# One more batch of block products with seven multiplications, four more pairs with float32 numerators, and other buffer limits in a planned attention and MoE kernel

## The chip, the cores and the metric

The kernel runs on one core of a Trainium2 chip. The metric is the time of one execution on the device in microseconds (us). TensorE (PE in the profile) multiplies matrices, VectorE (DVE), ScalarE (ACT) and GpSimd (POOL) do the elementwise work, and all large transfers are issued from the queue of SyncE (SP).

## The reference

For each of 8 batches and 8 heads (576 rows, 64 columns) the reference computes attention with random features, and passes the result, as 4608 tokens of 512 values, through two matrix products with an activation between them:

```python
proj = np.einsum('bhsd,md->bhsm', x, omega)          # q and k, 128 features
h = proj - sum(x * x) / 2;  phi = np.exp(h - max(h)) / np.sqrt(128)
kv = np.einsum('bhsm,bhsd->bhmd', k_p, v);  z = np.sum(k_p, axis=2)
num = np.einsum('bhsm,bhmd->bhsd', q_p, kv);  den = q_p . z + 1e-06
x = num / den                                        # 4608 x 512
h = x @ w_in                                         # 512 -> 2048
g = h * erf(log(1 + exp(h)))
out = g @ w_out                                      # 2048 -> 512
```

All of it is float32.

## The kernel before, in words

**Work.** Attention goes by pairs of heads, four pairs to a batch, numbered 0 to 31 (pair 4b + p is pair p of batch b; its tiles are called `..._b_p`). For a pair, TensorE projects keys (`ppk`) and queries (`ppq`), VectorE takes row maxima, ScalarE exponentiates into `fk` and `fq`, TensorE makes `kvp` (keys by values) from `fk`, and turns `fq` by three groups of transpositions (`pt`). The turned queries are copied out of PSUM to `qh`, the pair's key values to `kh`, and the products `nd` of both hold numerators and denominators, which are divided into `xs`.

From there the MoE part takes over, batch by batch. A batch has two phases of 1024 hidden columns; a phase has four granules of the first product (`h...`, 256 hidden columns each) and four column blocks of the second product (`o...`, 128 output columns each). A column block belongs to the phase before the one in whose span it stands, so the second product runs one phase behind the first.

**Split numbers.** Most products are made with float32r operands that are split into a high and a low part: a product then takes three matmuls (high by high, high by low, low by high). Weights lie in tiles `w` as pairs of parts, activations in `xh` and `xl`, gated values in `gh` and `gl`, turned queries in `qh` and `ql`, key values in `kh` and `kl`.

**First product, two forms.** In batches below `PLAIN` (lines 301 to 302 set it and `WHOLE`) `plain1` (line 609) makes a granule's four output blocks from two block products each: 8 block products of 6 matmuls, 48 in all, and each output is copied out of PSUM. From batch `PLAIN` on, `gemm1` (line 622) makes them from seven block products in Strassen's manner: 42 matmuls, and each block that leaves PSUM is added to others (`h_add`, line 960; 7 additions and one copy to a granule). That form needs sums of weight blocks, which `make_sums` (line 407) computes once, in the batch `PLAIN - 1`, from the tiles which are there anyway: it restores the whole weights (`R`), adds and subtracts blocks (`S`), splits the sums (`cS`) and stores them to DRAM, from where they are fetched as `wS`. It also needs differences of activation blocks (`xc`), made by `split` (line 545) at a batch's start.

**Numerators, two forms.** For pairs below `WHOLE`, `kh` and `qh` are plain float32, there are no low parts, and `nd` is one float32 matmul; from pair `WHOLE` on, they are split, and `nd` is three matmuls (`attend`, line 919).

**Weights.** The weights come packed as int64 and must be rebuilt once: each tile is loaded (`st`), shifted and joined on the engines (`wt`, `pw`), split into `w`, and stored (`wdw`). All later uses fetch it from DRAM. This happens in batch 0 for the first product, and one phase behind it for the second, so the last of it lies in the first half of batch 1.

**Order.** No loop of the program sets the order of the instructions. `build` writes a list of operations with due times, and `Plan.order` (line 134) simulates the engines with fixed costs and puts out one order for each of them; each engine then runs its own in order and waits on semaphores. Buffers are slots of pools (`SLOTS`, line 61), and `CAPS` limits how many slots of its pool a stream of tiles may hold at once: `st` for loaded weights and `S` (in the pool of `gl`, 6 slots), `wt` for half-made weights and `R` (in the pool of `gh`, 6 slots), `att` for the attention's PSUM tiles and `moe1`, `moe2` for those of the MoE products (8 PSUM slots together). The first four pairs have a limit of their own, 7.

```python
def weights1(b, ph, fp):                                  # lines 430 to 434
    if b < PLAIN:
        t0, t1 = (unit(("1", ph, 2 * fp + i)) for i in range(2))
        if b == PLAIN - 1:
            make_sums(ph, fp, t0, t1)
whole = n < WHOLE                                         # lines 497 and 508
if held[t.stream] + k >= (t.cap or caps.get(t.stream, 99)):   # in order()
    return False
(plain1 if b < PLAIN else gemm1)(b, ph, x)                # line 722
```

`PLAIN` also enters the due times of the phases (lines 334 and 716) and three limits: tiles `w` may take 6 of 8 slots, and `gh` and `gl` 4 of 6, until a phase that is named by `PLAIN`.

## Time and profile before

| | |
|---|---|
| median of three executions | 1088.04 us (1085.89 to 1089.02) |
| profiled execution | 1085.2 us, its span 1083.2 us |
| PE busy | 1066.8 us, 98% of the span |
| DVE, ACT, POOL busy | 724.0, 672.6, 462.6 us |
| moved by DMA | 231.27 MB, mean 213 GB/s |
| granted TensorE clock | 0.999 |

Busy times are unions of instruction spans. Matmuls overlap in their pipeline, so the mean of a matmul (298 ns) is longer than the distance from one to the next. A row of the timeline gives the start, the length, the engine, the source line (all operations of this kernel have the one line of a helper, L755, so that the tiles' names tell them apart), and in brackets how long the engine had been idle and for whom. The batches' spans, by the first matmul of their first granule, begin near 49, 172, 299, 435, 575 and 705 us, and then every 130 us.

### The profile page before, as it was taken

The page shows a single profiled execution, that of the slowest core. Times are in us where ns is not written, and L with a number is a line of the kernel's source. Part 1 is how long each engine was busy: PE and PEld are TensorE (multiplying, and loading weights), DVE is VectorE, ACT ScalarE, POOL GpSimd, SP SyncE. Part 2 cuts the span into 40 slices and gives each one's busy share as a digit, 9 for nine tenths or more (in the row PEclk, how much of TensorE's full clock was granted, in tenths as well). Part 3 has the DMA queues.
Part 4 walks back from the last instruction along what each step waited for, and adds up shares of the span by engine and source line. Part 5 has one row for each costly group of instructions (what it writes and reads, how often), then busy time and mean ns, then how long its engine had stood idle before and what let it go on. Part 6 is the DMA issues. An engine that isn't in the chain of part 4 may idle for free.

```text
span 1083.2 us, 21493 instructions
## 1 busy us (share of the span) xinstructions
PE 1066.8 (98%) x8272; PEld 1059.2 (98%) x8272; DVE 724.0 (67%) x1302; ACT 672.6 (62%) x1262; POOL 462.6 (43%) x362
## 2 busy tenths in 40 slices
PE   7899999999999999999999999999999999999998
PEld 7799999999999999999999999999999999999998
DVE  5999988683585676946667565766657757565541
ACT  7768876576676685647647555675556665564440
POOL 5436336352294673815335334452435412253300
PEclk9999999999999999999999999999999999999999
DMA  8465676676367676568765766667765766667771
GB/s 235 162 210 177 221 265 223 227 274 200 115 218 240 225 234 202 177 206 255 226 208 183 248 226 223 187 211 233 230 210 182 241 203 197 216 229 265 264 240 52
DMA packets 70117, 231.27 MB, mean 213 GB/s; under 512 B 8288, under 2 KB 8672, under 8 KB 70016
## 3 DMA queue, kind: packets, MB, share of 16 engines
q1 hardware_dynamic: 69952, 229.84, 64.9%
q8 instruction: 66, 1.08, 0.4%
q14 instruction: 35, 0.29, 0.1%
q0 software_dynamic: 64, 0.07, 0.0%
HBM read 195.26 MB, written 34.60 MB: 212 GB/s over the span
## 4 chain that ended last, share of the span: by engine, by line
PE 94%; DVE 4%; ACT 1%; issue 0%; DMA 0%; DVEq 0%; POOLq 0%
PE o L755 37%; PE h L755 14%; PE hS L755 12%; PE hA L755 9%; PE ppk L755 6%; PE ppq L755 6%; PE kvp L755 5%; PE nd L755 5%; PE pt L755 2%; DVE mxk L755 0%; DVE xl L755 0%; DVE pw L755 0%; DVE gl L755 0%; DVE xc L755 0%; DVE qh L755 0%
## 5 line engine op out<-in xcount | busy, mean ns | idle before, releaser
L755 PE MATMUL o<-gh,w 128*128 128x288 f32 x2048 | 442.3, 298 | 1.9 <-DVE ql L755 1.0
L755 PEld LDWEIGHTS o<-gh,w 128*128 128x128 f32 x2048 | 338.3, 188 | 2.5 <-PE o L755 1.2
L755 PE MATMUL o<-gl,w 128*128 128x288 f32 x1024 | 301.8, 295 | 0.0
L755 PEld LDWEIGHTS o<-gl,w 128*128 128x128 f32 x1024 | 192.7, 188 | 0.1
L755 PE MATMUL h<-xh,w 128*128 128x288 f32 x768 | 176.0, 303 | 0.6 <-DVE hs L755 0.6
L755 PE MATMUL hS<-xh,wS 128*128 128x288 f32 x640 | 160.0, 299 | 1.1 <-DVE u L755 1.1
L755 POOL TENSOR_TENSOR hs<-gs,hs 128x576 f32<-128x576 f32 x64 | 101.4, 1607 | 105.7 <-ACT gs L755 68.9
L755 POOL TENSOR_TENSOR gl<-hs,gh 128x576 fp32r<-128x576 f32 x66 | 117.9, 1810 | 33.0 <-ACT gh L755 25.7
L755 PEld LDWEIGHTS h<-xh,w 128*128 128x128 f32 x768 | 129.1, 188 | 1.5 <-DVE hs L755 0.8
L755 ACT ACTIVATE fk<-ppk,mxk 128x128 f32<-128x128 f32 x288 | 82.2, 375 | 74.8 <-DVE mxk L755 74.5
L755 PE MATMUL hA<-xh,w 128*128 128x288 f32 x480 | 122.8, 300 | 0.0
L755 ACT ACT_TABLE_LOAD x91 | 116.8, 1283 | 4.3 <-DVE hs L755 2.0
L755 PEld LDWEIGHTS hS<-xh,wS 128*128 128x128 f32 x640 | 112.9, 188 | 1.3 <-DVE u L755 1.3
L755 POOL TENSOR_TENSOR uq<-uq 64x576 f32<-64x576 f32 x42 | 49.7, 1201 | 150.3 <-DMA uq<-qT 105.3
L755 PE MATMUL h<-xl,w 128*128 128x288 f32 x384 | 113.0, 294 | 0.0
L755 ACT ACTIVATE fq<-ppq,mxq 128x128 f32<-128x128 f32 x288 | 81.6, 372 | 30.4 <-DVE mxq L755 30.2
L755 DVE TENSOR_REDUCE mxk<-ppk 128x3 f32<-128x384 f32 x96 | 52.4, 555 | 62.6 <-PE ppk L755 61.3
L755 PE MATMUL hS<-xl,wS 128*128 128x288 f32 x320 | 94.2, 294 | 0.0
L755 POOL TENSOR_TENSOR uk<-uk 64x576 f32<-64x576 f32 x46 | 52.4, 1159 | 86.1 <-DMA uk<-kT 60.8
L755 PEld LDWEIGHTS hA<-xh,w 128*128 128x128 f32 x480 | 85.5, 188 | 0.1
L755 DVE TENSOR_TENSOR os<-o,os 128x288 f32<-128x288 f32 x64 | 29.0, 455 | 83.5 <-PE o L755 83.5
L755 PE MATMUL ppk<-wk,uk 128*128 128x128 f32 x576 | 78.1, 280 | 4.1 <-DVE wk L755 4.0
(94 smaller groups left out, 2084.6 us busy)
## 6 DMA issues: line engine op xcount, KB each, us to landing
w<-wdw SPq DMA_DIRECT2D x184, 512.0 KB, 4.4
wS<-wdcS SPq DMA_DIRECT2D x80, 512.0 KB, 4.0
st<-w SPq DMA_DIRECT2D x32, 512.0 KB, 4.5
wdw<-w SPq DMA_DIRECT2D x32, 512.0 KB, 4.2
v<-vP SPq DMA_DIRECT2D x32, 325.0 KB, 3.6
w<-wdw SPq DMA_DIRECT2D x40, 256.0 KB, 3.5
out<-os SPq DMA_DIRECT2D x32, 288.0 KB, 3.5
uk<-kT SPq DMA_DIRECT2D x31, 288.0 KB, 3.8
```

The lines of the kernel that those rows point to most:

```text
L755: return tc.keep_in_program_order(method(*args, **kwargs))
```

## The change

Three constants are set to other values, and the limits of three streams. Batch 2 is computed with seven block products to a granule in place of eight, the sums of weights are made in batch 1 in place of batch 2, pairs 8 to 11 get float32 numerators, loaded and half-made weights may hold three slots each in place of two, and the attention four PSUM tiles in place of five.

```diff
-CAPS = dict(st=2, wt=2, cv=2, att=5, moe1=3, moe2=2)
+CAPS = dict(st=3, wt=3, cv=2, att=4, moe1=3, moe2=2)
...
-WHOLE = 8
-PLAIN = 3
+WHOLE = 12
+PLAIN = 2
```

Since a planner sets the order, these lines move instructions everywhere from the first 15 us on. Counted over the whole program, by form: PE has 48 MoE matmuls fewer and 32 `nd` matmuls fewer (for 16 `nd` products, one float32 matmul in place of three); DVE has 56 additions `hs` and `u` of batch 2 more, 12 `ql` and 8 `kl` fewer; SP has 16 fetches more (16 of `wS` with 512 KB and 8 of `w` with 256 KB more, 8 of `w` with 512 KB fewer). Three places show how rows moved.

DVE in batch 1, first phase, around the copy that empties a block of granule 0 (`h111_0_0`). Before:

```order
L755 CAST gh0_1_2_2223<-hs0_1_2_1587 128x1152
L755 COPY os0_3_2237<-o0_0_3_0_2111 128x288
L755 TENSOR_TENSOR gl0_1_2_2242<-hs0_1_2_1587,gh0_1_2_2223 128x1152
L755 COPY hs1_0_0_2252<-h011_0_0_2219 128x288
L755 TENSOR_TENSOR xs_2_0_2285<-nd_2_0_0_0_2209,rc_2_0_0_2257 64x288
L755 TENSOR_TENSOR xs_2_0_2285<-nd_2_0_1_0_2233,rc_2_0_0_2257 64x288
L755 COPY hs1_0_0_2252<-h111_0_0_2278 128x288
```

and now:

```order
L755 TENSOR_TENSOR R0_1_2205<-w1_0_3_28_2097 128x512
L755 TENSOR_REDUCE mxk_2_1_2232<-ppk_2_1_1_2228 128x3
L755 TENSOR_TENSOR S0_1_2259<-R0_1_2205 128x256
L755 TENSOR_REDUCE mxk_2_1_2232<-ppk_2_1_2_2255 128x3
L755 COPY qh_2_0_2284<-pt_2_0_0_2264 128x384
L755 TENSOR_TENSOR hs0_1_3_1876<-gs0_1_3_2055,hs0_1_3_1876 128x1152
L755 TENSOR_TENSOR S0_1_2259<-R0_1_2205,S0_1_2259 128x256
L755 COPY hs1_0_0_2203<-h111_0_0_2216 128x288
L755 TENSOR_TENSOR cS0_1_0_2324<-S0_1_2259,cS0_1_0_2324 128x2x256
```

Sums of weights (`R`, `S`, `cS`) now stand between the attention's maxima and copies of pairs 8 and 9 and the copies of batch 1's blocks; there is no `ql` row for pair 8.

PE at pair 10 (`_2_2`), in batch 1. Before, from the last transposition on (the first `nd` of the pair follows one matmul after these rows):

```order
L755 MATMUL pt_2_2_2_3121<-ident_67,fq_2_2_2793 128x128 x3
L755 MATMUL h001_1_1_3091<-xh1_1_1976,w1_1_2_43_2902 128x288
L755 MATMUL h001_1_1_3091<-xl1_1_2014,w1_1_2_43_2902 128x288
L755 MATMUL h001_1_1_3091<-xh1_1_1976,w1_1_2_43_2902 128x288
L755 MATMUL h001_1_1_3091<-xh1_0_1966,w1_1_2_43_2902 128x288
L755 MATMUL h001_1_1_3091<-xl1_0_1988,w1_1_2_43_2902 128x288
L755 MATMUL h001_1_1_3091<-xh1_0_1966,w1_1_2_43_2902 128x288
L755 MATMUL h011_1_1_3137<-xh1_0_1966,w1_1_2_43_2902 128x288
L755 MATMUL h011_1_1_3137<-xl1_0_1988,w1_1_2_43_2902 128x288
L755 MATMUL h011_1_1_3137<-xh1_0_1966,w1_1_2_43_2902 128x288
L755 MATMUL h001_1_1_3091<-xh1_1_1976,w1_1_2_43_2902 128x288
L755 MATMUL h001_1_1_3091<-xl1_1_2014,w1_1_2_43_2902 128x288
```

and now:

```order
L755 MATMUL kvp_2_2_2842<-v_2_2_2031,fk_2_2_2671 128x65 x4
L755 MATMUL ppk_2_3_0_2866<-wk_71,uk_2_3_2589 128x128 x3
L755 MATMUL ppk_2_3_1_2875<-wk_71,uk_2_3_2589 128x128 x3
L755 MATMUL ppk_2_3_2_2883<-wk_71,uk_2_3_2589 128x128 x3
L755 MATMUL pt_2_2_0_2888<-ident_67,fq_2_2_2818 128x128 x3
L755 MATMUL pt_2_2_1_2903<-ident_67,fq_2_2_2818 128x128 x3
L755 MATMUL pt_2_2_2_2913<-ident_67,fq_2_2_2818 128x128 x3
L755 MATMUL nd_2_2_0_0_2922<-qh_2_2_2899,kh_2_2_2870 128x288
L755 MATMUL o0_1_2_0_2925<-gh0_1_0_2127,w2_1_2_0_37_2805 128x288
```

The attention of pair 10 now stands in one piece, with no MoE matmul between transpositions and `nd`; pair 11 has a like place.

PE at pair 18 (`_4_2`), in batch 3. Before:

```order
L755 MATMUL pt_4_2_2_6381<-ident_67,fq_4_2_6087 128x128 x3
L755 MATMUL nd_4_2_0_0_6386<-qh_4_2_6363,kh_4_2_6159 128x288
L755 MATMUL nd_4_2_0_0_6386<-ql_4_2_6368,kh_4_2_6159 128x288
L755 MATMUL nd_4_2_0_0_6386<-qh_4_2_6363,kl_4_2_6170 128x288
L755 MATMUL nd_4_2_1_0_6400<-qh_4_2_6363,kh_4_2_6159 128x288
L755 MATMUL nd_4_2_1_0_6400<-ql_4_2_6368,kh_4_2_6159 128x288
L755 MATMUL nd_4_2_1_0_6400<-qh_4_2_6363,kl_4_2_6170 128x288
```

and now:

```order
L755 MATMUL pt_4_2_2_6378<-ident_67,fq_4_2_6113 128x128 x3
L755 MATMUL nd_4_2_0_0_6383<-qh_4_2_6362,kh_4_2_6155 128x288
L755 MATMUL nd_4_2_0_0_6383<-ql_4_2_6367,kh_4_2_6155 128x288
L755 MATMUL nd_4_2_0_0_6383<-qh_4_2_6362,kl_4_2_6166 128x288
L755 MATMUL hS43_1_0_6393<-xh3_0_5300,wS_1_0_1_131_6092 128x288
L755 MATMUL hS43_1_0_6393<-xl3_0_5328,wS_1_0_1_131_6092 128x288
L755 MATMUL hS43_1_0_6393<-xh3_0_5300,wS_1_0_1_131_6092 128x288
```

After these rows twelve more MoE matmuls follow before the second `nd` of the pair: 15 matmuls stand now between the two where none did.

## The prediction, as it was made before the run

> **What bounds the kernel now.** I read the page first, for the bound.

> ```profile
> span 1083.2 us, 21493 instructions
> PE 1066.8 (98%) x8272; PEld 1059.2 (98%) x8272; DVE 724.0 (67%) x1302; ACT 672.6 (62%) x1262; POOL 462.6 (43%) x362
> PE 94%; DVE 4%; ACT 1%; issue 0%; DMA 0%; DVEq 0%; POOLq 0%
> ```

> TensorE is busy for 98% of the span and holds 94% of the chain that ended last; DVE, the next one, has a third of the span free. Only 16.4 us are not PE's, so what shortens PE's own list shortens the kernel. Then the busy times by stretch, at the start, and by batch:

> ```profile
> 0.00:20.00 20.00, 15.85 (x105) 15.05 (x106) 8.08 (x20) 15.69 (x39) 11.43 (x17) 1.00 0.85 220
> 20.00:40.00 20.00, 17.15 (x127) 15.09 (x127) 19.40 (x40) 14.93 (x48) 8.84 (x10) 1.00 0.66 195
> 40.00:60.00 20.00, 18.52 (x146) 17.24 (x145) 19.16 (x40) 15.04 (x44) 9.68 (x12) 1.00 0.49 162
> ...
> 172.00:299.00 127.00, 127.00 (x998) 127.00 (x997) 80.89 (x140) 81.18 (x161) 49.09 (x39) 1.00 0.59 201
> 299.00:435.00 136.00, 136.00 (x1069) 136.00 (x1069) 93.67 (x142) 93.20 (x182) 86.76 (x70) 1.00 0.67 224
> 435.00:575.00 140.00, 137.34 (x1071) 136.36 (x1070) 94.84 (x169) 84.53 (x155) 66.11 (x45) 1.00 0.66 211
> 575.00:705.00 130.00, 130.00 (x1023) 129.98 (x1022) 85.93 (x167) 79.59 (x147) 53.68 (x39) 1.00 0.68 217
> ...
> 1005.00:1035.00 30.00, 30.00 (x230) 30.00 (x229) 14.12 (x29) 9.51 (x11) 8.99 (x6) 1.00 0.79 272
> ```

> Columns: stretch, length, busy PE, weight load, DVE, ACT, POOL (with counts), clock, DMA share, GB/s. PE's idle time lies in the first 60 us (4.15 + 2.85 + 1.48 = 8.5 us), in batch 3 (435 to 575: 2.7 us) and at the end; in batches 1, 2 and 4 it is zero. The clock is full, so no stretch hides a throttle. Last, what PE waited for, and where, by the waits and the timeline:

> ```profile
> PE ppk L755 <- DVE wk L755: 4.0, 1, 4.0
> PE nd L755 <- DVE qh L755: 1.9, 2, 1.0
> PE hS L755 <- DVE u L755: 1.1, 1, 1.1
> PE o L755 <- DVE ql L755: 1.0, 1, 1.0
> ...
> 21.27 2.22 PE L755 MATMUL kvp<-v,fk 128*128 128x130 f32 x18 [0.84 <-ACT fq L755]
> 27.44 0.72 PE L755 MATMUL nd<-qh,kh 128*128 128x288 f32 x2 [0.90 <-DVE qh L755]
> 28.86 0.97 PE L755 MATMUL nd<-qh,kh 128*128 128x288 f32 x3 [0.70 <-ACT fk L755]
> ...
> 444.08 0.37 PE L755 MATMUL o<-gh,w 128*128 128x288 f32 x1 [1.02 <-DVE ql L755]
> 452.93 0.40 PE L755 MATMUL hS<-xh,wS 128*128 128x288 f32 x1 [1.09 <-DVE u L755]
> 517.97 0.40 PE L755 MATMUL nd<-qh,kh 128*128 128x288 f32 x1 [0.18 <-ACT qh L755]
> 518.74 0.40 PE L755 MATMUL nd<-ql,kh 128*128 128x288 f32 x1 [0.37 <-DVE ql L755]
> ```

> Pair 1, early, runs its attention in one piece and PE waits three times, 2.4 us; later pairs have MoE matmuls between the links, and only pair 18 (at 518) still waits.

> **The products of batch 2.** Eight granules lose 6 matmuls each (42 in place of 48), so 48. In the stretch 1005 to 1035, where PE does nothing but such 288-column matmuls, 230 take 30 us: 0.1304 us each. 48 x 0.1304 = 6.3 us less on PE. Batches read whole say the same: batch 2 takes 136.0 us, batch 4, whose form it gets, 130.0.

> **The numerators of pairs 8 to 11.** Four pairs of four `nd` become one float32 matmul in place of three. What the float32 one costs is read where an early pair's stands in a full stream:

> ```profile
> 102.40 0.65 PE L755 MATMUL nd<-qh,kh 128*128 128x288 f32 x2
> 102.67 0.51 PE L755 MATMUL h<-xh,w 128*128 128x288 f32 x1
> 103.01 0.29 PE L755 MATMUL h<-xl,w 128*128 128x288 f32 x1
> ```

> The profile shows it as two records. From its start to that of the second matmul behind it are 0.61 us, of which one matmul is 0.13: 0.48 us, against 3 x 0.1304 = 0.39. So this part lengthens PE's list by 16 x 0.09 = 1.4 us. It takes work from DVE, in batch 1:

> ```profile
> L755 DVE TENSOR_TENSOR ql<-pt,qh 128x384 fp32r<-128x384 f32 x72 | 37.7, 549 | 1.7 <-ACT qh L755 1.2
> L755 DVE TENSOR_TENSOR kl<-kvp,kh 128x128 fp32r<-128x128 f32 x48 | 11.5, 281 | 0.6 <-ACT kh L755 0.5
> L755 DVE TENSOR_TENSOR hs<-hS,u 128x288 f32<-128x288 f32 x80 | 36.2, 452 | 6.2 <-PE hS L755 4.0 <-POOL xc L755 0.3
> L755 DVE TENSOR_TENSOR R<-w 128x512 f32<-128x512 f32 x12 | 13.5, 1124 | 2.7 <-DMA w<-wdw 2.6
> L755 DVE TENSOR_TENSOR cS<-S,cS 128x512 fp32r<-128x512 f32 x9 | 9.3, 1030 | 0.1
> L755 DVE TENSOR_TENSOR S<-R 128x256 f32<-128x256 f32 x8 | 7.0, 871 | 0.3
> ```

> 12 `ql` by 0.549 and 8 `kl` by 0.281 make 8.8 us. The work is hidden either way; its worth is the room.

> **The sums of weights, moved from batch 2 to batch 1.** On DVE the rows give 13.5 + 9.3 + 7.0 = 29.8 us, and 8 more instructions on `S`, in groups not shown, are an estimated 7 us at the same 0.87: some 36 us. POOL's part is read as a difference: batch 2 has 86.76 busy, batch 4 without sums 53.68, so 33 us. In batch 1 DVE then has 80.9 + 36 - 8.8 = 108 of 127 us, POOL 49 + 33 = 82, ACT 81.2 and a little. That is fuller than any stretch of that length except the start, and not full. On PE this counts zero; its cover is that DVE, without which the sums would be late, works 15% under the span.

> The sums wait for fetched weight tiles that the batch fetches anyway. Their 16 stores of 512 KB go through SP's queue; behind a store that waits for the sum stand loads of raw weights, fetches of `w` and loads for the next pairs. Before, such waits of the queue were paid in batch 2 with PE idle for nothing, and I take zero again. DMA has 201 GB/s in batch 1; 8.4 MB more over 127 us make 267, and the last stretch quoted has 272 with PE full. In batch 2 the 16 more fetches bring it to batch 4's traffic (217 GB/s).

> **The additions in batch 2.** 56 more on DVE at 0.452 are 25 us, and the sums' 36 us leave: DVE has less to do there than before. Batch 4 carries the form at 85.9 of 130 us without a wait, so zero.

> **The limits and the new order.** These cost nothing by themselves and move every wait. Two sides. Gone, as far as the order shows: at pair 18 the second `nd` now has 15 matmuls ahead of it, where it had none, which is 2 us of cover for the copies it waited for (0.18 + 0.37); and batch 3 is no longer the first of the new form, so that its first granule, with the waits at 444 and 453 (1.02 + 1.09), has other neighbours. Up to 2.7 us less. New: pairs 10 and 11 run their attention in one piece in batch 1, as pair 1 does. Bounds: nothing, if the first `nd`, which reads the first third of the turned queries alone, finds it copied; 2 x 2.4 = 4.9 us, if both wait as pair 1 does. I take half of it, 2.4 us, since only two of pair 1's three waits can occur (their keys were projected long ago). Batch 2 as the first batch of the new form may take over batch 3's waits; its cover, by the order, is like batch 4's, so zero, with 2.1 us as the other end. Sum of this part: -2.7 + 2.4, which I call zero, between -2.7 and +7.

> At the start, three slots for loaded weights put one 512 KB load on SP's queue ahead of the keys of pair 3:

> ```profile
> 15.07 0.47 SPq L755 DMA_DIRECT2D uk<-kT x1
> ...
> 35.03 2.23 PE L755 MATMUL ppk<-wk,uk 128*128 128x128 f32 x18
> ...
> st<-w SPq DMA_DIRECT2D x32, 512.0 KB, 4.5
> ```

> The keys are asked for at 15.07 and projected at 35.03; a load of 4.5 us fits between, so zero.

> **Sum.** 1085.2 - 6.3 + 1.4 + 0 = 1080.3 us for an execution like the profiled one. That one lies 2.8 us under the median (1088.04), so a median of 1083.1 us, between 1080.4 and 1090.1 by the bounds above.

> **Rival 1, the waits eat it (no change).** Pairs 10 and 11 wait in full, as pair 1 did, and nothing else goes: 1088.04 - 4.9 + 4.9 = 1088.0. For it: three early waits at such places. Against it: these pairs are float32 now, without the `ql` and `kl` that other pairs wait for, and DVE was at 19.4 of 20 us in pair 1's stretch, which batch 1 does not reach.

> **Rival 2, batch 1 chokes (slower).** In the first half of batch 1 the second product's weights are still being made, on DVE and POOL, and now half of the sums come on top. Sums slow each other:

> ```profile
> 303.38 1.75 POOL L755 TENSOR_TENSOR R<-w 128x512 f32<-128x512 f32 x1
> ...
> 303.89 1.79 DVE L755 TENSOR_TENSOR R<-w 128x512 f32<-128x512 f32 x1
> ...
> L755 DVE TENSOR_TENSOR R<-w x12: 678/726/1920, 290.6 to 408.1; 128x512 f32<-128x512 f32 x12
> ```

> The DVE sum that began inside POOL's took 1.79 us and ended after it; the shortest of its kind took 0.678. If sums and weight making run into each other, the block copies on DVE behind them come late, the 3 PSUM tiles of the first product stay taken, and PE waits. Priced by the nearest waits (1.02 and 1.09 us): one for each of the 8 groups of sums and for 1 in 2 of the 8 weight tiles, 12 x 1.05 = 12.6 us, so 1088.04 - 4.9 + 12.6 = 1095.7; it decides from about 8 waits on (8.2 us, 3.3 more than the gain). For it: these rows. Against it: batch 2 had 93.67 us on DVE and 86.76 on POOL with the same sums in them, and PE did not idle.
> [...]

> **Rival 3, more than the count (faster).** The waits at 444, 453 and 518 go, and no new one comes: 1088.04 - 4.9 - 2.7 = 1080.4. For it: batches 4 and 5, whose order batch 3 now shares, have none.

> That the change does not do what it says is excluded: the order has the 48 matmuls fewer.

> **Chances.** The forecast 0.52, rival 1 0.17, rival 2 0.14, rival 3 0.17. About 0.3% (3.3 us) is what a measurement of this kernel tells from no change. The forecast's cases spread over some 2 us around -4.9, so four fifths of them pass -3.3 (0.41), the rest is "same" (0.11); with rival 3 faster has 0.58; same gets 0.11 and most of rival 1 (0.14), 0.25; slower has rival 2 and the rest of rival 1, 0.17. The range goes from 1078.5, a little under rival 3, to 1090, which holds rival 1 and the upper bound of the sum, and leaves rival 2 out; the forecast's own range is 1080.4 to 1086.

> **What would show it.** PE's busy time falls by about 5 us, to 1062, and batch 2 takes 130 to 131 us. PE's waits show nothing at pair 18 and the start of batch 3, and about 1 us each at `nd` of pairs 10 and 11. DVE in batch 1 has 105 to 115 us. I am wrong if PE's idle time grows by more than 3 us, and rival 2 is right if it does so in batch 1, on block copies or weight tiles.

## The result: 1.8% slower

| | before | after |
|---|---|---|
| median | 1087.68 us (1085.89 to 1089.02) | 1106.62 us (1104.13 to 1110.20) |
| ratio, 95% interval | | 1.0181, 1.0165 to 1.0198 |
| profiled execution, its span | 1085.2, 1083.2 us | 1110.2, 1108.4 us |

The prediction was 1083.1 us; the kernel takes 18.9 us more than before by the medians. The profiled execution of the changed kernel lies 3.6 us above its median and that of before 2.5 us under its own, so some 6 of the 25.2 us between the two spans belong to the two executions.

The page of the changed kernel:

```profile
span 1108.4 us, 21429 instructions
PE 1075.2 (97%) x8208; PEld 1059.9 (96%) x8208; DVE 752.1 (68%) x1334; ACT 693.6 (63%) x1277; POOL 405.0 (37%) x331
PE 87%; DVE 8%; ACT 2%; DMA 2%; issue 1%; POOL 0%; SPq 0%; DVEq 0%
```

PE has 64 records fewer, as counted, and yet is busy 8.4 us longer; it is idle 33.2 us where it was 16.4. Busy times by stretch (columns as in the prediction) show where:

```profile
20.00:40.00 20.00, 17.68 (x112) 16.26 (x111) 15.97 (x31) 15.21 (x43) 10.70 (x12) 0.83 0.81 221
40.00:60.00 20.00, 16.83 (x109) 14.98 (x108) 17.95 (x35) 13.75 (x42) 5.88 (x8) 0.91 0.36 126
60.00:100.00 40.00, 38.64 (x296) 37.70 (x297) 32.55 (x58) 25.47 (x56) 17.49 (x18) 1.00 0.63 209
100.00:120.00 20.00, 16.28 (x108) 15.19 (x107) 18.13 (x31) 18.62 (x33) 12.36 (x9) 0.91 0.50 171
...
177.00:269.00 92.00, 86.91 (x652) 83.08 (x650) 77.28 (x112) 70.19 (x144) 51.24 (x41) 1.00 0.62 214
269.00:322.00 53.00, 53.00 (x407) 52.74 (x405) 35.73 (x48) 33.64 (x57) 19.36 (x16) 1.00 0.80 263
322.00:345.00 23.00, 19.32 (x133) 18.14 (x133) 22.83 (x31) 15.19 (x29) 14.42 (x9) 0.93 0.58 190
345.00:464.00 119.00, 119.00 (x935) 119.00 (x935) 72.45 (x144) 74.24 (x133) 39.54 (x31) 1.00 0.69 226
```

Four places are new or worse: the start, the end of batch 0 (100 to 120), the first half of batch 1 (177 to 269) and the first granule of batch 2 (322 to 345). The rest of batch 2 is full. The clock, full before, is 0.83 to 0.93 in three of these. What PE waited for, in total, times and longest:

```profile
PE nd L755 <- DVE ql L755: 3.2, 4, 0.9
PE nd L755 <- ACT qh L755: 2.7, 3, 1.8
PE hA L755 <- DVE os L755: 2.6, 1, 2.6
PE ppq L755 <- POOL gl L755: 2.4, 1, 2.4
PE kvp L755 <- ACT fq L755: 2.2, 2, 1.7
PE o L755 <- ACT w L755: 2.2, 1, 2.2
```

Apart from the 4.0 us for `wk`, which both kernels have, these are the six largest; before had 0.4 us for `ql`, 0.2 us for a `qh` of ScalarE, 0.8 us for `fq`, and none of the other three. There is no single large wait, but 28 of up to 2.6 us (before: 12 of up to 1.1 us), for different engines.

**How the loss is counted.** Orders differ, so stretches at equal times hold different work. I therefore took each matmul of the order, gave it the distance to the next that its kind has where nothing waits in these traces (0.132 us with 288 columns, 0.484 for a float32 `nd` in two records, 0.110 to 0.112 for a record of the small ones), and compared the sum up to a matmul with the time at which it started. The difference, **lost time**, is waiting and slow clock together. By this count PE's own work fell from 1058.0 to 1053.1 us, 4.9 us as predicted. Lost time rose from 21.0 to 51.2 us. Between the start of batch 4 and the end, before, it grows by 0.8 us in some 500, so the distances are good to 0.2%.

Lost time by place, for the profiled execution of each kernel, in us. "Start" ends with granule 1 of batch 0; a batch's halves are its phases:

| kernel | median | ratio to before, 95% | start | rest of b. 0 | b. 1, 1st half | b. 1, 2nd | b. 2, granule 0 | rest of b. 2 | b. 3 | b. 4 to 7 | all |
|---|---|---|---|---|---|---|---|---|---|---|---|
| before | 1087.68 | | 13.8 | 2.0 | 0.1 | 0.1 | 0.1 | 0.2 | 4.0 | 0.8 | 21.0 |
| the change | 1106.62 | 1.0165 to 1.0198 | 23.1 | 5.9 | 7.4 | 0.1 | 6.3 | 0.4 | 1.6 | 6.3 | 51.2 |
| 1 forms only | 1117.12 | 1.0257 to 1.0290 | 14.8 | 2.6 | 24.0 | 0.2 | 1.4 | 0.1 | 2.1 | 12.9 | 58.1 |
| 2 limits only | 1099.84 | 1.0091 to 1.0135 | 18.5 | 6.0 | 0.1 | 0.1 | 1.4 | 0.2 | 4.6 | 4.5 | 35.4 |
| 3 forms, third slot | 1119.59 | 1.0273 to 1.0326 | 16.7 | 3.8 | 14.4 | 0.2 | 5.3 | 1.8 | 4.8 | 15.8 | 62.8 |
| 4 forms, att 4 | 1111.75 | 1.0205 to 1.0248 | 15.6 | 7.6 | 13.0 | 0.3 | 8.2 | 0.8 | 1.7 | 6.2 | 53.4 |
| 5 seven products only | 1116.93 | 1.0232 to 1.0281 | 18.0 | 2.0 | 16.8 | 0.8 | 7.4 | 1.1 | 1.5 | 14.4 | 62.0 |
| 6 float32 pairs only | 1087.97 | 0.9987 to 1.0015 | 13.6 | 1.2 | 0.5 | 0.1 | 0.0 | 0.1 | 4.0 | 0.7 | 20.3 |
| 7 sums in own slots | 1107.55 | 1.0148 to 1.0193 | 13.2 | 1.2 | 10.3 | 0.4 | 6.8 | 0.5 | 1.7 | 13.7 | 47.9 |
| 8 sums left out, stored | 1108.50 | 1.0163 to 1.0215 | 15.7 | 2.7 | 11.5 | 4.3 | 1.4 | 0.1 | 2.1 | 15.4 | 53.2 |
| 9 no sums, no stores | 1108.04 | 1.0165 to 1.0217 | 14.0 | 2.6 | 7.1 | 0.1 | 2.4 | 2.7 | 6.2 | 12.7 | 48.0 |
| 10 as 9, `xc` later | 1100.47 | 1.0108 to 1.0142 | 14.2 | 2.7 | 0.5 | 0.0 | 2.3 | 4.2 | 3.4 | 11.5 | 38.7 |
| 11 forms, other order | 1084.88 | 0.9974 to 0.9993 | 15.5 | 5.0 | 0.2 | 0.2 | 2.7 | 0.2 | 0.9 | 1.1 | 25.8 |
| 12 old form, other order | 1094.20 | 1.0053 to 1.0083 | 15.5 | 6.7 | 0.0 | 0.1 | 0.0 | 0.2 | 5.3 | 1.2 | 29.0 |
| 13 change, slots freed | 1098.15 | 1.0085 to 1.0124 | 18.3 | 5.9 | 3.5 | 0.1 | 6.5 | 0.8 | 0.1 | 1.9 | 37.0 |
| 14 forms, freed, att split | 1098.71 | 1.0080 to 1.0117 | 16.2 | 2.6 | 4.7 | 4.3 | 8.9 | 1.7 | 0.3 | 2.0 | 40.6 |

Each run has its own runs of the kernel before beside it (medians 1086.6 to 1087.7 us); the ratios are to those.

### The profile page after: what moved, and what is told of

It is laid out like the page before. It is cut to its first block, busy times and chain, and to the rows that moved or that the text cites. A ratio compares the mean times of both kernels' runs of the same rounds, so it can differ in the third digit from the quotient of the medians.

```text
span 1108.4 us, 21429 instructions
## 1 busy us (share of the span) xinstructions
PE 1075.2 (97%) x8208; PEld 1059.9 (96%) x8208; DVE 752.1 (68%) x1334; ACT 693.6 (63%) x1277; POOL 405.0 (37%) x331
## 4 chain that ended last, share of the span: by engine, by line
PE 87%; DVE 8%; ACT 2%; DMA 2%; issue 1%; POOL 0%; SPq 0%; DVEq 0%
PE o L755 35%; PE hS L755 13%; PE hA L755 10%; PE h L755 8%; PE kvp L755 5%; PE ppq L755 5%; PE ppk L755 5%; PE nd L755 4%; PE pt L755 2%; DVE gl L755 1%; DMA uq<-qT 1%; DVE pw L755 1%; DVE hs L755 1%; DVE gh L755 1%; DVE mxk L755 1%
## 5 line engine op out<-in xcount | busy, mean ns | idle before, releaser
L755 PE MATMUL o<-gh,w 128*128 128x288 f32 x2048 | 444.0, 299 | 4.4 <-ACT w L755 2.2
L755 PEld LDWEIGHTS o<-gh,w 128*128 128x128 f32 x2048 | 337.9, 188 | 7.7 <-ACT w L755 2.7
L755 PE MATMUL o<-gl,w 128*128 128x288 f32 x1024 | 301.7, 295 | 0.0
L755 PE MATMUL hS<-xh,wS 128*128 128x288 f32 x768 | 194.6, 302 | 0.0
L755 PEld LDWEIGHTS o<-gl,w 128*128 128x128 f32 x1024 | 192.7, 188 | 0.3
L755 POOL TENSOR_TENSOR hs<-gs,hs 128x576 f32<-128x576 f32 x60 | 94.8, 1603 | 216.7 <-ACT gs L755 202.4
L755 PE MATMUL hA<-xh,w 128*128 128x288 f32 x576 | 144.1, 299 | 3.5 <-DVE os L755 2.6
L755 PEld LDWEIGHTS hS<-xh,wS 128*128 128x128 f32 x768 | 136.4, 189 | 0.0
L755 ACT ACTIVATE fk<-ppk,mxk 128x128 f32<-128x128 f32 x288 | 83.3, 375 | 71.7 <-DVE mxk L755 71.4
L755 ACT ACTIVATE fq<-ppq,mxq 128x128 f32<-128x128 f32 x288 | 83.1, 373 | 54.6 <-DVE mxq L755 54.2
L755 PE MATMUL h<-xh,w 128*128 128x288 f32 x512 | 116.1, 305 | 0.3 <-DVE qh L755 0.3
L755 PE MATMUL hS<-xl,wS 128*128 128x288 f32 x384 | 113.6, 296 | 0.0
L755 PEld LDWEIGHTS hA<-xh,w 128*128 128x128 f32 x576 | 102.1, 189 | 4.1 <-DVE os L755 2.8
L755 POOL TENSOR_TENSOR gl<-hs,gh 128x576 fp32r<-128x576 f32 x50 | 82.4, 1668 | 38.0 <-ACT gh L755 28.3
L755 DVE TENSOR_REDUCE mxk<-ppk 128x3 f32<-128x384 f32 x96 | 53.2, 555 | 60.0 <-PE ppk L755 58.4
L755 ACT ACTIVATE gh<-hs 128x1152 fp32r<-128x1152 f32 x54 | 62.8, 1171 | 49.4 <-DVE hs L755 20.9
L755 PEld LDWEIGHTS h<-xh,w 128*128 128x128 f32 x512 | 85.7, 189 | 1.3 <-DVE qh L755 0.6
L755 POOL TENSOR_TENSOR uk<-uk 64x576 f32<-64x576 f32 x50 | 58.0, 1180 | 78.7 <-DMA uk<-kT 49.1
L755 PE MATMUL ppk<-wk,uk 128*128 128x128 f32 x576 | 81.3, 288 | 4.2 <-DVE wk L755 4.0
L755 PE MATMUL hA<-xl,w 128*128 128x288 f32 x288 | 85.0, 295 | 0.0
L755 ACT ACTIVATE rc<-nd,eps 64x288 f32<-64x288 f32 x128 | 63.6, 497 | 33.4 <-PE nd L755 30.9
## 6 DMA issues: line engine op xcount, KB each, us to landing
w<-wdw SPq DMA_DIRECT2D x176, 512.0 KB, 4.4
wS<-wdcS SPq DMA_DIRECT2D x96, 512.0 KB, 4.3
st<-w SPq DMA_DIRECT2D x32, 512.0 KB, 4.5
wdw<-w SPq DMA_DIRECT2D x32, 512.0 KB, 3.7
```

Of the source, the lines that this page charges most:

```text
L755: return tc.keep_in_program_order(method(*args, **kwargs))
```

## The experiments

### Forms and limits apart

**Run 1, forms only.**

```diff
-WHOLE = 8
-PLAIN = 3
+WHOLE = 12
+PLAIN = 2
```

> The new forms (seven products from batch 2 on, twelve float32 pairs) with the limits of before. Theory L (the limits lengthened the kernel, the start above all): the first granule of batch 0 begins at 49 us as before, TensorE keeps its full clock until 116 us and beyond, and the median falls at least 12 us below that of the changed kernel, to 1094 or less; if the limits are all of the loss, 1083. Theory F (batches 1 and 2 choke on the moved sums, whatever the limits): the losses of about 6.5 us in the first half of batch 1 and 6.4 us in the first granule of batch 2 stay, 1093 to 1096. Theory F alone, with nothing from the limits, would leave it at 1104 or more.

1117.12 us: without the new limits the forms are slower still, by 30.5 us. 24.0 us are lost in the first half of batch 1, where PE waits (in total, times, longest; 176 to 285 us) for tiles `w` of the second product:

```profile
PE o L755 <- ACT w L755: 7.6, 3, 2.7
PE o L755 <- DVE w L755: 2.8, 3, 1.2
PE h L755 <- ACT fk L755: 2.3, 1, 2.3
```

**Run 2, limits only.**

```diff
-CAPS = dict(st=2, wt=2, cv=2, att=5, moe1=3, moe2=2)
+CAPS = dict(st=3, wt=3, cv=2, att=4, moe1=3, moe2=2)
```

> The limits of the change (three slots for loaded weights, four PSUM tiles for the attention) with the forms of before. Theory L: the start loses 9 us as in the changed kernel (first granule of batch 0 at 56 us), the second half of batch 0 another 5 us, so 1100 to 1104. Theory F: within 3 us of before, 1085 to 1091, since no sum is moved.

1099.84 us, 13.2 us slower, with the arithmetic of before. The loss lies at the start (+4.7), in batch 0 (+4.0) and in batches 4 to 7 (+3.7); batch 1 is untouched. So the limits do cost by themselves; and since they cost 13.2 us with the old forms and take 10.5 us off with the new ones, the two parts of the change can't be added up.

**Runs 3 and 4, one limit each,** with the forms of run 1: `st=3`, and `att=4`.

```diff
-CAPS = dict(st=2, wt=2, cv=2, att=5, moe1=3, moe2=2)
+CAPS = dict(st=3, wt=2, cv=2, att=5, moe1=3, moe2=2)
```

```diff
-CAPS = dict(st=2, wt=2, cv=2, att=5, moe1=3, moe2=2)
+CAPS = dict(st=2, wt=2, cv=2, att=4, moe1=3, moe2=2)
```

> The new forms and of the limits only that for loaded weights (three slots), four PSUM tiles taken back to five. Theory L, if the loss at the start is the slot's: the half-made third weight tile stands on ScalarE ahead of a copy of pair 1's turned queries and waits for its load about 3 us, PE idles, its clock is halved for 7 to 10 us before 60 us, and the first granule of batch 0 begins at 55 to 57 us: 8 to 10 us above the run with the forms alone. Rival: the start is lost by the PSUM limit, then this one begins at 49 us.

> The new forms and of the limits only that for the attention's PSUM tiles (four). Theory L, start lost by the weight slot: the first granule of batch 0 begins at 49 us; with four tiles pairs 16, 20, 24 have 2.2 us of matmuls between transposition and numerators instead of 0.6, so batches 4 to 7 lose at most 1 us each; the time is within 4 us of the run with the forms alone. Rival: start at 56 us.

1119.59 and 1111.75 us. Four attention tiles add 5.0 us in batch 0 and halve the loss of batches 4 to 7 (6.2 against 12.9). Both also have less loss than run 1 in the first half of batch 1 (13.0 and 14.4 against 24.0) and more in the first granule of batch 2, so neither limit acts in one place alone. The start with the third loaded-weight slot (16.7 against 14.8 in run 1) differs by less than two executions of one order do (4.6, below), so its size is not settled by run 3. The third slot for half-made weights does nothing: with `wt=3` the order is the same, row by row, as with `wt=2`.

**Runs 5 and 6, one form each.** In run 5 `PLAIN` alone is 2, in run 6 `WHOLE` alone is 12, both with the limits of before.

```diff
-PLAIN = 3
+PLAIN = 2
```

```diff
-WHOLE = 8
+WHOLE = 12
```

> Only the seven products from batch 2 on (eight float32 pairs, limits of before). Theory S (the sums of weights in the first half of batch 1 hold the slots and tiles that the making of the second product's weights needs): the loss of the forms stays, at least 18 us between the first granules of the two phases of batch 1, 1110 to 1120. Rival W (the float32 pairs are what hurts, by reordering the attention of batch 1): within 5 us of before.

> Only the twelve float32 pairs (seven products from batch 3 on, limits of before). By my price of a float32 matmul, 16 x 0.09 = 1.4 us on TensorE: 1087 to 1090, by both theories except W, by which it is 1100 or more.

1116.93 and 1087.97 us. The loss is that of the seven products; the float32 pairs change nothing that can be measured (interval 0.9987 to 1.0015). PE's counted work is 1059.5 us there, 1.5 more than before, as the prediction's 1.4.

### What seven products in batch 2 do to batch 1

**Run 7: sums in slots of their own.** `R` shares the stream `wt` with half-made weights, and `S` the stream `st` with loaded ones. A stream gives its slots in the order of its list, so a load that stands behind an `S` can't start before that sum has its slot. Run 7 has the forms of run 1 and gives both their own limit, in the same pools:

```diff
-        r = pl.tile("gh", f"R{ph}_{fp}", [P, 2, 2, BW], F32, "wt")
+        r = pl.tile("gh", f"R{ph}_{fp}", [P, 2, 2, BW], F32, "sumr", 1)
-        s = pl.tile("gl", f"S{ph}_{fp}", [P, 4, BW], F32, "st")
+        s = pl.tile("gl", f"S{ph}_{fp}", [P, 4, BW], F32, "sums", 1)
```

> The new forms with the limits of before, but the tiles of the sums (R and S) count in streams of their own, one slot each, in the same pools: loads of raw weights and half-made weights then have both of their slots for themselves. Theory S in its narrow form (the slots): the loss in the first half of batch 1 falls from 24 us to under 10, TensorE's waits on w there from 10 us to under 3, and the time to 1105 or less. Rival T (VectorE and GpSimd have no time for the sums, or they lock each other): the loss stays within 4 us of 24, 1113 to 1121.

1107.55 us: the first half of batch 1 loses 10.3 us in place of 24.0, and PE waits 1.5 us for `w` there in place of 10.4. The loss and the time are a little above what was expected, but more than half of that loss is the shared stream.

**Run 8: sums left out.** The forms of run 1, with plain tiles stored where the sums would be.

```diff
-        r = pl.tile("gh", f"R{ph}_{fp}", [P, 2, 2, BW], F32, "wt")
...
+            store(("S", ph, fp, i), t)
```

> The new forms with the limits of before, without the sums of weights: the tiles of plain weights are stored in their place, with the same transfers, and the products of batches 2 to 7 use them, so the output is another one. Theory S in its wide form (slots, tiles and engines that the sums take in batch 1): the loss in the first half of batch 1 falls from 24 us to under 4; the later batches keep theirs, about 11 us, so 1092 to 1100. If the loss stays over 15 us, the sums are not its cause, but the new order of the attention.

1108.50 us, and still 11.5 us lost in the first half of batch 1. That is no less than in run 7 (10.3), where all of that work is done. So the work of the sums on DVE and POOL is not shown to cost anything there; that part of my theory fell. Two things of the new form were left in batch 1: the 16 stores, and the differences of activation blocks. These are made by `split` for batch 2, in a tile `xc` which lies in the pool of `gl`:

```python
xc = pl.tile("gl", f"xc{b}_{c}", [P, 4, T], F32, "xc", 1)
for i, (x, y) in enumerate(((b12, b11), (b22, tt(0)), (b22, b12), (b21, tt(1)))):
```

The first difference reads pair 8 alone, so the tile may be taken as soon as that pair is divided; the others wait for pair 10. In the pool of 6 slots, `gl` may hold 4 in batch 1 and `st` 2. With `xc` there, one load of weights may find no slot.

**Runs 9 and 10: without stores, and with `xc` taken later.** Both have the forms of run 1 and neither sums nor stores; run 10 has this line more:

```diff
-            for i, (x, y) in enumerate(((b12, b11), (b22, tt(0)), (b22, b12), (b21, tt(1)))):
+            for i, (x, y) in ((2, (b22, b12)), (0, (b12, b11)), (1, (b22, tt(0))), (3, (b21, tt(1)))):
```

> The forms of the change (PLAIN 2, WHOLE 12) with the limits of before; the sums of weights are neither made nor stored, batch 2 and later fetch the plain tiles in their place (so the output is another one). Batch 1 then has the work it had before, and of the new form only the activation differences: their first tile (xc2_0) may be taken from the six gl slots as soon as pair 8 is divided, at 191 to 219 us in the runs so far, and is held until 317 to 328 us, through the stretch in which the second product's weights are loaded into the same slots (st). Theory A (that slot): the first half of batch 1 still loses 5 to 12 us, on o waiting for w, with no sum in the program; total 1100 to 1109. Theory B (the 16 stores of the run before, on SP's queue): the first half of batch 1 loses under 3 us.

> As the run with neither sums nor stores (output again another one), with one line more: of the four differences the first to be made is the one that reads both pairs 8 and 10, so that the tile xc2_0 is taken some 30 to 50 us later, when pair 10 is divided. Theory A: the first half of batch 1 loses under 3 us, 5 to 10 us less than in that run. Theory B: no difference between the two in batch 1. The waits at pairs 16, 20 and 24 (3 to 5 us each with five PSUM tiles for the attention) stay under both; total about 1097 to 1102.

1108.04 and 1100.47 us. The order of four subtractions is worth 7.6 us. With it the first half of batch 1 loses 0.5 us, without it 7.1, of which 2.4 us are waits for `w`. The rows of the first difference, and of the 8 loads of raw weights in batch 1 (count, ns, start of the first and of the last), of run 9:

```profile
L737 POOL TENSOR_TENSOR xc<-xs x1: 812/812/812, 187.6 to 187.6; 128x288 f32<-128x288 f32 x1
L737 SPq DMA_DIRECT2D st<-w x8: 332/333/465, 175.7 to 237.4; - x8
```

and of run 10, where another difference is now the first and takes the tile at 255.8:

```profile
L737 DVE TENSOR_TENSOR xc<-xs x1: 458/458/458, 256.5 to 256.5; 128x288 f32<-128x288 f32 x1
L737 SPq DMA_DIRECT2D st<-w x8: 332/333/1077, 175.9 to 223.0; - x8
```

The last load is asked for at 223.0 in place of 237.4. The same row of before and of the changed kernel, where `xc` is taken at 218.7 and both causes are at work:

```profile
L755 SPq DMA_DIRECT2D st<-w x8: 332/333/902, 171.9 to 223.7; - x8
```

```profile
L755 DVE TENSOR_TENSOR xc<-xs x1: 460/460/460, 218.7 to 218.7; 128x288 f32<-128x288 f32 x1
L755 SPq DMA_DIRECT2D st<-w x8: 328/345/847, 186.8 to 261.6; - x8
```

The changed kernel asks for its last raw tile 38 us later than before, though for the first of the eight only 15 us later. PE waits for the fifth of them (`w2_1_2_0`), which is asked for at 233.3, and before at 199.8. The second row is that wait:

```profile
244.25 0.75 PE L755 MATMUL nd<-qh,kh 128*128 128x288 f32 x2 [0.53 <-ACT qh L755]
247.22 0.40 PE L755 MATMUL o<-gh,w 128*128 128x288 f32 x1 [2.21 <-ACT w L755]
```

Runs 9 and 10 keep the waits of pairs 16, 20, 24 and 28, which all runs have that combine seven products from batch 2 on with five attention tiles throughout and the pair length and lead of before (11.5 to 15.8 us in batches 4 to 7; in run 10, three waits of 2.8 us and 1.7 us of slow clock, shown in the last section, are 10 of them). These repeat with each batch, since the order does; why the planner puts these `nd` right behind their transpositions under `PLAIN` 2 and not under 3 was not taken apart.

**Run 13: the same on the change itself.** Its limits stay; `R` and `S` have their own limits, as in run 7, and `xc` is taken later, as in run 10.

> The change itself, with its own limits, and two edits: R and S in streams of their own (one slot each in the same pools), and xc2_0 taken only when pair 10 is divided. Slot theory: of the 7.3 us that the changed kernel loses in the first half of batch 1 at least 5 go, and the last raw weight tile of the second product is asked for before 245 us (261.6 in the changed kernel); the start (9.3 us) and the second half of batch 0 (about 5 us) stay; time 1097 to 1103. If the loss in batch 1 comes from something else in the changed kernel (its limits or the one-piece attention of pairs 10 and 11): no change there, 1104 to 1110.

1098.15 us, 8.5 us under the changed kernel. The first half of batch 1 loses 3.5 us in place of 7.4, a little less gain than the 5 us expected, and the last load is at 237.9 us. Of what is left there, 2.1 us are pair 10, which waits for its turned queries between its first and its second `nd`. The waits in batches 4 to 7 went too, which was not expected.

**Run 14: all named causes at once.** Forms of the change, limits of before, the slots as in run 13, and four attention tiles from pair 12 on only:

```diff
-        return EARLYB if n < NP else None
+        return EARLYB if n < NP else 4 if n >= 12 else None
```

> All forms of the change with the limits of before (two slots for loaded weights, five attention tiles), the same two edits for the slots, and four attention PSUM tiles from pair 12 on only. If the limits cost the start and batch 0, and the slots batch 1: the loss up to batch 1 is within 3 us of before, batch 1 loses under 4 us, batches 4 to 6 at most 1.6 us each; what then remains is the first granule of batch 2 (6 to 7 us in the run with slots of their own). Time 1092 to 1098. If the start's loss isn't from the third slot or the attention limit, the time is over 1100.

1098.71 us. The start and batch 0 are within 3.0 us of before, and batches 4 to 7 lose 2.0 us, as expected; but the two halves of batch 1 lose 9.0 us and the first granule of batch 2 8.9, more than expected. With each cause removed the order is another one, and waits of 1 to 3 us come up at other places. Taking away causes one by one does not lead back to the 21 us of before.

### The forms under another order

**Runs 11 and 12.** So I asked whether any order gets the 5 us. Run 11 has all forms, with six settings of the order changed; they were picked for an early end of the planner's own schedule. Run 12 differs from it in `PLAIN` alone.

```diff
-CAPS = dict(st=2, wt=2, cv=2, att=5, moe1=3, moe2=2)
+CAPS = dict(st=2, wt=2, cv=2, att=5, moe1=3, moe2=3)
-PAIR = 8.6
+PAIR = 8.8
-LEAD = 30.0
+LEAD = 25.0
-              plan=clock[0] + 10.0, size=P * HW * 8)
+              plan=clock[0] + soon, size=P * HW * 8)   # 30 for sums, 10 for the rest
-        r = pl.tile("gh", f"R{ph}_{fp}", [P, 2, 2, BW], F32, "wt")
+        r = pl.tile("gh", f"R{ph}_{fp}", [P, 2, 2, BW], F32, "sumr", 2)
-        s = pl.tile("gl", f"S{ph}_{fp}", [P, 4, BW], F32, "st")
+        s = pl.tile("gl", f"S{ph}_{fp}", [P, 4, BW], F32, "sums", 1)
-        return EARLYB if n < NP else None
+        return EARLYB if n < NP else 4 if n >= 12 else None
```

> All of the forms (seven products from batch 2, sums in batch 1, twelve float32 pairs), with the order made under other settings: R has two and S one slot limit of their own, the sums' stores are due 30 us after their phase's time in place of 10, four attention PSUM tiles from pair 12 on and five before, three PSUM tiles for the second product, pair length 8.8 in place of 8.6 and lead 25 in place of 30. Theory A (the forms are worth their 5 us, and the waits that ate them are those of one order): waits and half clock together cost 18 to 28 us against the 21 of before, and the time is 1080 to 1090. Rival (sums in batch 1 cost PE time in any order): over 1095.

> The same settings of the order as in the run with all forms and another order, with PLAIN 3 and twelve float32 pairs: the difference between the two is batch 2 with its seven products alone. Theory A: 3 to 8 us slower than that run (the count says 6.3). Rival: faster than that run, since sums in batch 1 cost more than they bring in any order.

1084.88 us (1084.05 to 1086.44): faster than before by 2.1 us (0.9983, 0.9974 to 0.9993), and 21.7 us under the changed kernel with the same arithmetic. Run 12 takes 1094.20, so under this order the seven products of batch 2 are worth 9.3 us: 6.3 by count, and 3.2 of lost time (29.0 against 25.8 in the profiled executions). The settings were picked for the forms of run 11 and not for those of run 12, which is 7 us slower than the kernel before; best order against best order, the forms bring the 2.1 us. The page of run 11 and two of its stretches:

```profile
PE 1064.0 (98%) x8208; PEld 1052.9 (97%) x8208; DVE 735.6 (68%) x1314; ACT 669.9 (62%) x1259; POOL 459.7 (42%) x374
...
172.00:240.00 68.00, 68.00 (x527) 67.09 (x525) 56.29 (x85) 50.00 (x97) 46.50 (x40) 1.00 0.66 232
299.00:345.00 46.00, 44.21 (x344) 43.43 (x344) 35.67 (x57) 34.74 (x58) 28.91 (x21) 1.00 0.67 216
```

In the first half of batch 1 PE is not idle at all, with the sums on DVE and POOL, which are 83% and 68% busy. In the first granules of batch 2 it is idle for 1.8 us.

## Why the prediction was wrong

**Products and numerators: right.** -6.3 and +1.4 were predicted, -4.9 together. PE's counted work fell by 4.9, and run 6 has the +1.4 to +1.5 alone. The claim that PE's busy time would be 1062 was wrong (1075.2): busy time holds the slow clock too, 17 us at half of it (below).

**"The limits and the new order. These cost nothing by themselves": the step that failed.** It was priced between -2.7 and +7, and chosen as zero. Alone (run 2) the limits cost 13.2 us, and with the forms the new order loses 30.2 us more than before in the profiled execution. I priced the waits that I could see in rows of before (pairs 10, 11 and 18, batch 3). Those came out as said or smaller: batch 3 loses 1.6 in place of 4.0, pair 18 waits no more, and pairs 10 and 11 wait 0.5 and 0.3 us for their copies, so rival 1 has its place right and not its size. But some 21400 instructions were put in a new order, and the price of that isn't in the two or three places at which one looks.

The kernel holds a better price, which the prediction did not use. `Plan.order` keeps the end of its simulated schedule (`self.span`): 1095.8 us for the kernel before and 1114.9 for the changed one, 19.1 more, where 18.9 was measured. For eleven of the fourteen runs, too, its difference from before is within 3 us of the measured one; runs 9, 10 and 12 took some 6 us more than it says. Its costs are fixed and know no clock, so that it meets the number so closely is in part luck.

**"A load of 4.5 us fits between, so zero": wrong at the start.** I compared the load with the keys of pair 3, and not with the engines that work on what it brings. ScalarE's timeline in the changed kernel:

```profile
29.37 0.66 ACT L755 ACTIVATE wt<-st 128x512 f32<-128x512 f32 x1 [3.07 <-DMA st<-w]
31.21 0.49 ACT L755 ACTIVATE qh<-pt 128x384 f32<-128x384 f32 x1 [1.17 <-PE pt L755]
```

The third loaded tile is taken up by ScalarE, which stands 3.07 us for it. That wait itself costs nothing: PE is busy meanwhile (6.80 of the 6.80 us from 24.2 on, last section), and ScalarE's next copy still waits 1.17 us for PE (in runs 2 and 13, which have the same order on all engines through most of batch 0, 2.09 and 0.80 us). The cost comes later, on VectorE, where all three steps of that tile's `pw` now stand ahead of the copy of pair 2's turned queries; before, one of them did. DVE's rows of the last step and of the copy, and PE's two waits:

```profile
42.15 0.69 DVE L755 SCALAR_TENSOR_TENSOR pw<-st,pw 128x512 int32<-128x512 int32 x1
43.21 1.01 DVE L755 COPY qh<-pt 128x384 f32<-128x384 f32 x2
```

```profile
43.81 2.25 PE L755 MATMUL nd<-qh,kh 128*128 128x288 f32 x8 [1.51 <-DVE qh L755]
49.14 2.22 PE L755 MATMUL kvp<-v,fk 128*128 128x130 f32 x18 [1.07 <-DVE xs L755]
```

Runs 2 and 13 have the same two waits, 1.51 and 1.07 us. Run 3, which differs from run 1 in this slot alone, has them with 1.43 and 1.07 us, and run 1 has neither. The start lost 23.1 us in this execution, and 18.5 and 18.3 in runs 2 and 13, so some 4.6 us of the 9.3 are the order's, and as much came with this one execution (it has 10.2 us at half clock there, and each of those 3.4). The four kernels with the third slot lose 16.7 to 23.1 us at the start, the other twelve 13.2 to 18.0.

**The sums: zero by occupancy was the wrong measure.** "Its cover is that DVE, without which the sums would be late, works 15% under the span" asks whether an engine has time. It has: PE runs full beside the sums in run 11, at 83% of DVE, and waits without any sum in run 9. What was short was slots. The sums came into the streams of the weight loads, and the activation differences (which I had not listed as moved at all: `split` for batch 2 now makes `xc` in batch 1) into their pool. The description of the limits told of it: `R` and `S` are named there beside the tiles whose slots they share.

**The first granule of batch 2: mis-sized.** I named it ("batch 2 as the first batch of the new form may take over batch 3's waits") with zero and 2.1 us as ends. It lost 6.3. DVE is busy 22.83 of 23 us there: beside the new form's differences and splits it had the last two `cS` of the sums, late from batch 1:

```profile
L755 DVE TENSOR_TENSOR gl<-hs,gh 128x1152 fp32r<-128x1152 f32 x4 | 5.8, 1493 | 0.0
L755 DVE TENSOR_TENSOR cS<-S,cS 128x512 fp32r<-128x512 f32 x2 | 3.1, 1540 | 0.0
```

The `os` copy stands in DVE's list behind the last of these. DVE's timeline there, and PE's, which waits 2.56 us for the copy:

```profile
335.57 1.63 DVE L755 TENSOR_TENSOR cS<-S,cS 128x512 fp32r<-128x512 f32 x1
337.13 0.75 DVE L755 CAST gh<-hs 128x1152 fp32r<-128x1152 f32 x1
337.80 0.44 DVE L755 COPY os<-o 128x288 f32<-128x288 f32 x1
```

```profile
338.29 0.61 PE L755 MATMUL hA<-xh,w 128*128 128x288 f32 x1 [2.56 <-DVE os L755]
```
Without sums (runs 9 and 10) this granule loses 2.3 to 2.4 us. But the late `cS` alone can't be the cause: run 1 has its last one at 337.8, 3 us into the same granule, with DVE busy 21.69 of 23 us, and loses 1.4; and before, the first 23 us of batch 3 (435 to 458), where the new form began, had DVE busy for 22.47, with PE idle for 2.1 us where it is 3.7 now. Which of DVE's rows stands ahead of the copy that PE waits for decides, and what set that order stays open.

**Rival 2** had the sign, and one of its places: a loss in batch 1, on weight tiles. Its price (12.6 us in batch 1) is above the 7.4 lost there, and its mechanism is not what was found. By the sign that I named for it, it was right: PE's idle time grew by 16.8 us, and of the 5.1 us in batch 1 (177 to 322) 3.3 are waits for weight tiles. Single sums do run long beside POOL's work: before, an `R` on DVE takes 0.68 to 0.76 us in seven of its twelve rows, and 1.30 to 1.92 in the five that overlap instructions of POOL by 0.75 us or more. But no run needs that for the loss: run 9, without any sum, loses 7.1 us in the first half of batch 1, and run 11, with all of them, 0.2.

**The other signs.** DVE in batch 1 has 113 us (105 to 115 said). Batch 2 takes 142.0 us (322 to 464) and not 130 to 131; 6.7 of them are lost, and what other work the order put into it was not taken apart. One reading of the kernel before was short: 1.4 us of PE's idle time lie in batch 0, between 120 and 172 us.

## What to carry to other kernels

- Where a planner sets an in-order list, an edit that "only" moves work is a new schedule. On a kernel whose bound engine waits 2% of its time, don't price it at zero; compare the planner's own ends before and after (19.1 us here), and look for the spread: one set of forms took 1084.9 to 1119.6 us here under eight orders, a spread seven times the gain that was counted.
- Ask of moved work which slots it takes and how long it keeps them, not only whether its engine has time. One tile taken 68 us early, by the order of four subtractions, cost 7.6 us.
- Judge a form by the best order for each side. Runs 11 and 12, in an order picked for the form, gave the seven products 9.3 us; run 5, in an order made for something else, gave them a loss of 29; the best of either side are 2.1 us apart.

## What the runs showed of the hardware that was not expected

**Half clock after short waits.** Before, the granted clock is full (1.00) up to the last 1.7 us. After, it is at half for 24.2 to 31.0, 51.5 to 54.9, 116.3 to 119.7 and 338.2 to 341.6 us, 17.0 us in all, which cost at most 8.5 us of PE time. The first of these, by the busy times of stretches, and the wait ahead of the third, by the timeline:

```profile
24.20:31.00 6.80, 6.80 (x33) 6.80 (x33) 4.46 (x10) 2.69 (x7) 2.53 (x4) 0.50 1.03 242
```

```profile
116.40 1.83 PE L755 MATMUL ppq<-wq,uq 128*128 128x128 f32 x7 [2.37 <-POOL gl L755]
```

PE had not been idle for long ahead of it, nor ahead of the fourth (2.56 us, above). Run 10 has one wait four times, at pairs 16, 20, 24 and 28. Its timeline at the first three:

```profile
454.47 0.40 PE L737 MATMUL nd<-qh,kh 128*128 128x288 f32 x1 [2.77 <-DVE ql L737]
587.36 0.61 PE L737 MATMUL nd<-qh,kh 128*128 128x288 f32 x1 [2.77 <-DVE ql L737]
721.37 0.40 PE L737 MATMUL nd<-qh,kh 128*128 128x288 f32 x1 [2.78 <-DVE ql L737]
```

and 3.4 us from about there on (the second stretch begins 0.56 us ahead of its matmul, where the clock falls):

```profile
454.50:457.90 3.40, 3.40 (x25) 3.37 (x26) 2.40 (x6) 2.28 (x6) 2.25 (x2) 1.00 0.03 7
586.80:590.20 3.40, 2.84 (x12) 2.84 (x13) 2.99 (x8) 1.38 (x4) 1.55 (x2) 0.50 0.02 5
721.40:724.80 3.40, 3.40 (x25) 3.37 (x26) 2.39 (x6) 2.27 (x6) 2.25 (x2) 1.00 0.00 0
```

```profile
450.24:453.65 3.41, 1.46 (x14) 1.18 (x12) 3.41 (x4) 2.84 (x9) 2.03 (x2) 1.00 0.81 258
583.36:586.77 3.41, 1.23 (x12) 0.96 (x10) 3.41 (x5) 2.63 (x9) 1.80 (x1) 1.00 0.72 238
716.48:719.89 3.41, 2.11 (x18) 1.78 (x17) 3.41 (x3) 3.40 (x10) 2.69 (x2) 1.00 0.92 307
719.89:723.30 3.41, 1.93 (x14) 1.90 (x15) 3.38 (x8) 1.41 (x5) 1.00 (x1) 1.00 0.13 28
```

PE is idle for 1.95, 2.18, 1.30 and 1.48 us of these, and the clock falls after the second. Over all intervals of the sixteen traces that are at full clock (the last two of each left out), each of the 33 with 1.98 us or more of idle PE is followed by half clock, none of the 4911 with less than 1.06 us, and 15 of the 95 between. What decides among those was not found. In these traces waits of 2.4 to 2.8 us were enough for the clock to fall, some of the time, and 1.98 us of idle time in one interval every time. In run 10 the wait that ends at 587.36 so cost up to 1.7 us more than its own 2.77 (half of the 3.4 us that follow), and after the three others the clock stayed at 1.00. This may be one reason why single executions of one order differ: of the changed kernel's four, that of 1104.13 us has a mean clock of 0.997, and those of 1106.19 to 1110.20 have 0.992 or 0.993.
